# Sorted block attention and a PReLU FFN: unpadded q for batches 1 to 3, identity products up to the first FFN product, three banks for V of batch 0

## The chip, the cores and the metric

The kernel runs on one core of one Trainium2 chip. The metric is the device time of one launch in microseconds (us). TensorE is called PE, its weight loads PEld, VectorE DVE, ScalarE ACT, GpSimd POOL, and SyncE SP.

## The reference

There are 4 batches, 8 heads, 768 tokens and head size 64; tokens fall into 8 blocks of 96. A sorting matrix of 8 x 8 for each batch and head mixes the blocks of k and v; each block of q then attends to its own mixed block. The result, 3072 tokens of 512, goes through an FFN of width 2048.

```python
for _ in range(5):                       # P = sort_net, 8 x 8 per batch and head
    P = np.exp(P - np.max(P, axis=-1, keepdims=True))
    P = P / (np.sum(P, axis=-1, keepdims=True) + 1e-09)
    P = P / (np.sum(P, axis=-2, keepdims=True) + 1e-09)
k_sorted = np.einsum('bhij,bhjcd->bhicd', P, k_b)
v_sorted = np.einsum('bhij,bhjcd->bhicd', P, v_b)
scores = scale * np.matmul(q_b, k_sb.transpose(0, 1, 2, 4, 3))
attn = softmax(scores)
x = np.matmul(attn, v_sb)                # then to tokens x 512
h = x @ w_in                             # 3072 x 512 by 512 x 2048
g = np.maximum(h, 0.0) + alpha * np.minimum(h, 0.0)
return (g @ w_out).astype(np.float32)
```

## The kernel before

**Work in groups.** A group g is one block of one batch: g = 8 b + i, 32 groups in all, each with 8 heads. Batch 0 and the others ("far") go different ways. For each group `attention` issues: a score product of the 8 heads into the two psS banks (`s1`), a row maximum on DVE (into `nf` or `nm`), the exponential on ACT, an output product with V and a column of ones (`o`, into psO), a reciprocal and a multiplication on DVE (`xq`), and a turn of the result into `xT`. Group 1 uses psH and psYP in place of psS and psO. In batch 0 the scores are computed a second time with the operands exchanged, so that the exponential comes out turned already, and `xq` is turned on PE (`tr`). In the far batches the exponential `Esb` is turned into `ET` by a DMA transpose on SP's queue, and `xq` into `xT` by another.

**Operands.** `KT` holds the mixed k with 64 features of four heads in rows 0 to 63 and of the other four in rows 64 to 127. `prep_k` and `prep_v` mix k and v by products with the block matrix `BDK`, and copies on ACT or DVE empty the banks; `conv_v` first brings v into `VD`. q of batch 0 is brought into `QTz[0]` by `prep_q`. q of the far batches is loaded by eight POOL DMAs (`load_q`) into `QN`, in which each head has 128 columns, 64 with data and 64 of zeros, written once by eight POOL memsets; six DMA transposes (`turn_q`) of 128 x 1024 bring it into `QTz`, with 768 columns for each head. A far score product thus has 128 rows, of which 64 are zero, and 96 columns of weights; a score product of batch 0 has 64 rows and 128 columns of weights, of which the last 32 belong to the next block.

**FFN.** `ffn1` makes one of 16 parts of the hidden layer for up to four groups: four products into a psH bank, Relu on ACT, one DVE operation into `hT`. `ffn2` makes 128 tokens of output from `hT`, copies them to `outstg` and stores them from SP's queue. FFN work stands between the groups and fills PE.

**Order.** Nothing is ordered by hand. Every operation is entered with its engine, a planned duration, the keys that it reads and writes and a priority. `schedule` plays the operations through in planned time, `search` repeats this 1500 times with some priorities shifted at random and keeps the shortest plan, and `emit` writes each engine's instructions in that fixed order, with waits for what they need. A wait holds whatever stands behind it on the same engine.

**Filler.** After the plan is made, `fill` goes along PE's order and puts identity products into the gaps that the plan shows, 0.9 of each gap by the filler's unit (215 ns for a product of 512 columns). Their result in bank psY is not used. There are two stretches: from 5 us of planned time to the first V product that uses psY, and from the first FFN product to the first product of `ffn2`. A filler product waits for the identity matrix and stands in PE's order as any other.

```python
n = int((op.start - begin) * 0.9 / unit)
if op.start <= hi and n > 0:
    x = _Op("pe", lambda e, n=n: make(e, n), n * unit, 0.0, None, len(self.ops))
```

Of the lines that the profile names: L372 is any copy on ACT or DVE, L401 the loads of q, L409 its turns, L449 the memsets of `QN`, L515 the product that spreads the sorting matrices, L542 the products of q and k preparation, L565 the copy that pads `KT`, L585 those of V preparation, L622 the far scores, L625 the scores of batch 0 and L646 and L637 their second pass, L631 the row maximum, L658 the far exponential, L663 and L694 the DMA transposes to `ET` and `xT`, L669 the exponential of batch 0, L678 the output products, L686 `xq`, L701 its turn on PE, L723, L733 and L736 the first FFN layer on PE, ACT and DVE, L762 the second, L776 the stores, L877 the filler.

Of the kernel before, what the change touches and what calls it, by code (L numbers as in the profile page):

```python
# [24 lines left out]
BK0 = BLK + 16  # L25
NE = 3
# [34 lines left out]
class _Graph:  # L61
# [141 lines left out]
    def fill(self, make, unit, first, spans):  # L203

        out, last = [], self.ops[first].end + 300
        for op in self.order["pe"]:
            for lo, hi in spans:
                begin = max(last, lo)
                n = int((op.start - begin) * 0.9 / unit)
                if op.start <= hi and n > 0:  # L210
                    x = _Op("pe", lambda e, n=n: make(e, n), n * unit, 0.0, None, len(self.ops))
                    x.start, x.end = begin, begin + n * unit
                    x.deps.add(first)
# [76 lines left out]
def bass_sinkhorn_attn__then__act_prelu_kernel(  # L290
# [48 lines left out]
    QN = sb("QN", [128, 6, 8, 128], BF16)  # L339
# [3 lines left out]
    QTz = [sb("QTz%d" % n, [128, 2, 4, S], BF16) for n in range(2)]  # L343
# [51 lines left out]
    def load_q(b, prio):  # L395
        if b == 0:
            G.add(POOL, lambda e: e.dma_start(QS[0][:, :], AP(q.tensor, 0, [[3072, 128], [1, 3072]])),
                  load_us, w=[("QS", 0)], prio=prio, dma=(d_q[0], 0))
            return
        for h in range(H):  # L400
            G.add(POOL, lambda e, h=h: e.dma_start(  # L401
                AP(QN, h * 128 + (h // 4) * 64, [[6144, 128], [1024, 6], [1, 64]]),
                AP(q.tensor, b * HB + h * S * D, [[D, 128], [128 * D, 6], [1, D]])),
                660, r=[("QN0", h)] + paced(13, h // 2) * (b == 3), w=[("QN", h)], prio=prio,
                dma=(d_qn[h], 0))

    def turn_q(b, t, prio):
        n = b % 2
        G.add(SYNC, lambda e: e.dma_start_transpose(  # L409
            AP(QTz[n], t * 128, [[6144, 128], [768, 8], [1, 128]]),  # L410
            AP(QN, t * 1024, [[6144, 128], [1, 1024]])),
            4500, r=[("QN", h) for h in range(H)] + [("turned", 8 * b - 8 + t)] * (b > 1),
            w=[("QTzt", n, t)] + ([("Q0", u) for u in range(6)] + ["QTtail"] if n == 0 and t == 0 else []),
            prio=prio, dma=(d_qt[t], 0))
# [16 lines left out]
    def consts():  # L431
# [9 lines left out]
        G.add(DVE, lambda e: e.memset(AP(QTz[0], 3072, [[6144, 128], [1, 32]]), 0.0), 80, w=["QTtail"], prio=-60)  # L441
        G.add(DVE, lambda e: e.memset(AP(KT[0], 4 * NB * BK0, [[4 * NB * BK0 + 16, 128], [1, 16]]), 0.0), 80,
              w=["KTtail"], prio=-60)
        for n in range(2):
            G.add(DVE, lambda e, n=n: e.memset(AP(Es0[n], 768, [[800, 112], [1, 32]]), 0.0), 80, w=[("Etail", n)], prio=-60)
        for n in range(NE):
            G.add(DVE, lambda e, n=n: e.memset(AP(ET[n], 768, [[800, 128], [1, 32]]), 0.0), 80, w=[("ETtail", n)], prio=-21)
        for h in range(H):
            G.add(POOL, lambda e, h=h: e.memset(  # L449
                AP(QN, h * 128 + (1 - h // 4) * 64, [[6144, 128], [1024, 6], [1, 64]]), 0.0),  # L450
                400, w=[("QN0", h)], prio=-21)
# [96 lines left out]
    def prep_q(u, prio, bank):  # L548
        t, off, row, keys = bank
        G.add(PE, pairs(QS[0], 0, u, identb, 0, 128, bank), 372, r=[("QS", 0), "identb"], w=keys, prio=prio)  # L550
        o = AP(QTz[0], 8 * u, [[6144, 128], [96, 32], [48, 2], [1, 8]])
        i = AP(t, off, [[row, 128], [2, 32], [1, 2], [64, 8]])
        G.add(EITHER, lambda e: copy(e, o, i), t_either(512), r=keys, w=[("Q0", u)], prio=prio)
# [14 lines left out]

    first_y = []
# [7 lines left out]
    def prep_v(b, u, prio, bank=BANK_P):  # L577
        t, off, row, keys = bank
        n = b % 2

        def f(e):
            inst = None
            for dd in range(8):
                for th in range(2):
                    inst = e.matmul(AP(t, th * 64 * row + off + dd * 64, [[row, 64], [1, 64]]),  # L585
                                    AP(VD, (8 * u + dd) * 64, [[4096, 128], [1, 64]]),
                                    AP(BDK, b * 128 + th, [[512, 128], [2, 64]]))
            return inst
        op = G.add(PE, f, 374, r=[("VD", u), "VD0", ("BDK", b)], w=keys, prio=prio)
        if keys == ["psY"]:  # L590
            first_y.append(op)
        o = AP(VS[n], 8 * u, [[64 * 65, 112], [65, 64], [1, 8]])
        i = AP(t, off, [[row, 112], [1, 64], [64, 8]])
        G.add(EITHER, lambda e: copy(e, o, i), {"act": 685, "dve": 690}, r=keys + [("VS1", n)], w=[("VS", n, u)],
              prio=prio)

    d_e = [dma_sem("e%d" % n) for n in range(NE)]
    d_x = [dma_sem("x%d" % n) for n in range(NE)]

    def attention(g, prio):  # L600
# [14 lines left out]
        def s1(e):  # L615
            inst = None
            for h4 in range(4):
                for hp in range(2):
                    p = pos(h4, hp)
                    o = AP(psX, (p // 4) * 512 + (p % 4) * 96, [[1024, 96 if far else 128], [1, 96]])  # L620
                    if far:
                        inst = e.matmul(o, AP(QTz[n], hp * 3072 + h4 * 768 + i * 96, [[6144, 128], [1, 96]]),  # L622
                                        AP(KT[n], (h4 * 8 + i) * bk, [[ld, 128], [64, 2], [1, 48]]))
                    else:
                        inst = e.matmul(o, AP(QTz[n], hp * 64 * 6144 + h4 * 768 + i * 96, [[6144, 64], [1, 128]]),  # L625
                                        AP(KT[n], hp * 64 * ld + (h4 * 8 + i) * bk, [[ld, 64], [64, 2], [1, 48]]))
            return inst
        G.add(PE, s1, 395, r=kt_keys + qt_keys + [("xq", 1)] * (g == 2),
# [12 lines left out]
        def s2(e):  # L641
            inst = None
            for h4 in range(4):
                for hp in range(2):
# [3 lines left out]
                             AP(QTz[n], hp * 64 * 6144 + h4 * 768 + i * 96, [[6144, 64], [1, 96]]),  # L648
# [17 lines left out]
        else:  # L666
            G.add(PE, s2, 700, r=kt_keys + qt_keys + [("nm", m), "identb"],
                  w=banks_s, prio=ps_)
            G.add(ACT, lambda e: e.activation(  # L669
                AP(Es0[m], 0, [[800, nk], [384, 2], [1, 384]]),  # L670
                AP(psX, 0, [[1024, nk], [512, 2], [1, 384]]),
                ACTF.Exp), t_act(768), r=banks_s, w=[("Es0", m)], prio=ps_)

# [8 lines left out]
        G.add(PE, o, t_pe(*[(65, 65)] * 8), r=vs_keys + ([("ET", me), ("ETtail", me)] if far else [("Es0", m), ("Etail", m)]), w=banks_o, prio=prio)  # L682
# [111 lines left out]
    for u in range(8):  # L794
        prep_v(0, u, -45, (BANK_O + [BANK_P, BANK_Y])[u % 4])
# [78 lines left out]
    def warm(e, n):  # L874
        inst = None
        for _ in range(n):
            inst = e.matmul(psYP[:, 0, :], identb[:, :], AP(identb, 0, [[128, 128], [0, 4], [1, 128]]))  # L877
        return inst
    G.fill(warm, 215, ident_op, [(5000, first_y[0].start), (ffn_ops[0].start + 1, ffn_ops[1].start)])
# [40 lines left out]
```

## Time and profile before

| | |
|---|---|
| median of 3 runs | 254.17 us (253.9 to 256.3) |
| the profiled execution, its own time | 255.69 us |
| its span, first to last instruction | 254.0 us |
| PE busy | 235.3 us, 2679 products |
| DVE, ACT, POOL busy | 171.5, 160.5, 38.5 us |
| mean granted clock of PE | 0.987 |
| bytes moved | 32.17 MB |

The profile is of one execution; its span leaves out what lies before the first and after the last instruction. Busy time of PE counts overlapped products once each stretch, and products are pipelined, so the price of a group of products is read from its start to the start of the next. The granted clock is that of the throttle, 1.00 for full speed.

### The profile page before, as it was taken

How to read it: one execution, taken by the hardware profiler on the slowest of the kernel's cores; microseconds unless marked ns; L12 is line 12 of the kernel's file. 1: busy time of each engine (PE TensorE's matmuls, PEld its weight loads, DVE VectorE, ACT ScalarE, POOL GpSimd, SP SyncE). 2: the span in 40 equal slices, each digit the busy share in tenths (PEclk: the TensorE clock that was granted, in tenths of full speed). 3: DMA queues.
4: the chain of work that ended last, by engine and by line, in shares of the span. 5: the costliest groups of instructions: out<-in, count | busy, mean ns of one | idle time of the engine just before them, and what ended most of it. 6: DMA issues, size and time to landing. Idle time of an engine off the chain costs nothing.

```text
span 254.0 us, 6423 instructions
## 1 busy us (share of the span) xinstructions
PE 235.3 (93%) x2679; PEld 140.7 (55%) x2679; DVE 171.5 (68%) x347; ACT 160.5 (63%) x429; POOL 38.5 (15%) x63
## 2 busy tenths in 40 slices
PE   4796899989997978989899999999999999999995
PEld 1455678657654544556555555555555555555554
DVE  5887668796856775977885666656667765645530
ACT  4475446598866765878866485766677457534531
POOL 8995000000360011037000000000000000000000
PEclk9999589999999999999999999999999999999999
DMA  5999999999999999999979345233234433311103
GB/s 102 211 211 203 181 215 166 216 188 187 101 159 106 172 162 143 220 146 183 94 158 149 67 115 130 50 90 85 71 70 122 80 66 88 90 58 40 43 5 122
DMA packets 75534, 32.17 MB, mean 127 GB/s; under 512 B 67808, under 2 KB 71152, under 8 KB 75504
## 3 DMA queue, kind: packets, MB, share of 16 engines
q0 software_dynamic: 23632, 13.63, 41.1%
q1 hardware_dynamic: 51872, 18.11, 38.7%
q8 instruction: 21, 0.34, 0.6%
q14 instruction: 9, 0.07, 0.1%
HBM read 27.28 MB, written 6.29 MB: 132 GB/s over the span
## 4 chain that ended last, share of the span: by engine, by line
PE 75%; DVE 12%; DMA 9%; ACT 2%; issue 1%
PE psH L723 29%; PE psYP L762 26%; DMA ET<-Esb 8%; PE psS L762 3%; PE psO L678 3%; PE psS L622 3%; PE psYP L585 3%; PE psYP L542 2%; DVE hT L736 2%; DVE VD L372 2%; DVE VS L372 1%; PE psYP L877 1%; PE psS L637 1%; DVE KT L372 1%; ACT Esb L658 1%
## 5 line engine op out<-in xcount | busy, mean ns | idle before, releaser
L736 DVE SCALAR_TENSOR_TENSOR hT<-t,omaT,psH 128x384 bf16<-128x384 f32 (+1 forms) x139 | 77.5, 572 | 39.7 <-ACT t L733 38.1
L723 PE MATMUL psH<-xT,w_in_bf 128*128 128x384 bf16 (+1 forms) x556 | 98.5, 314 | 1.6 <-DVE hT L736 1.3
L733 ACT ACTIVATE t<-psH 128x384 f32<-128x384 f32 (+1 forms) x139 | 62.8, 466 | 44.5 <-PE psH L723 41.4
L762 PE MATMUL psYP<-w_out_bf,hT 128*128 128x512 bf16 x336 | 83.9, 379 | 1.0 <-DVE hT L736 0.6
L723 PEld LDWEIGHTS psH<-xT,w_in_bf 128*128 128x128 bf16 x556 | 50.8, 99 | 35.0 <-DVE hT L736 7.8
L658 ACT ACTIVATE Esb<-psS,nf 96x96 bf16<-96x96 f32 x192 | 46.3, 345 | 2.1 <-DVE nf L631 2.1
L762 PEld LDWEIGHTS psYP<-w_out_bf,hT 128*128 128x128 bf16 x336 | 30.7, 98 | 29.7 <-DVE hT L736 0.7
L401 POOL DMA_DIRECT2D QN<-in_q_dram x24 | 20.0, 857 | 45.2 <-DMA QTz<-QN 44.5
L631 DVE TENSOR_REDUCE nf<-psS 96x8 f32<-96x768 f32 x24 | 22.7, 948 | 3.9 <-PE psS L622 3.9
L686 DVE TENSOR_TENSOR xq<-psO,rec 96x512 bf16<-96x512 f32 x31 | 21.3, 686 | 1.0
L372 ACT ACTIVATE VS<-psYP 112x512 bf16<-112x512 f32 x17 | 11.7, 689 | 6.3 <-PE psYP L585 6.2
L372 ACT ACTIVATE outstg<-psYP 128x512 f32<-128x512 f32 x15 | 9.0, 597 | 9.9 <-PE psYP L762 9.8
L585 PE MATMUL psYP<-BDK,VD 128*64 128x64 bf16 x448 | 12.4, 198 | 1.9 <-DVE hT L736 1.0
L683 DVE RECIPROCAL rec<-psO 96x8 f32<-96x8 f32 x31 | 6.2, 201 | 11.7 <-PE psO L678 11.7
L877 PE MATMUL psYP<-identb 128*128 128x512 bf16 x34 | 10.6, 451 | 3.4 <-ACT identb L372 3.4
L585 PEld LDWEIGHTS psYP<-BDK,VD 128*64 128x64 bf16 x448 | 9.3, 111 | 6.9 <-issue 1.8
L622 PEld LDWEIGHTS psS<-KT,QTz 128*96 128x96 bf16 x192 | 11.7, 124 | 2.5
L678 PEld LDWEIGHTS psO<-VS,ET 112*128 112x128 bf16 x192 | 8.6, 98 | 7.6 <-DMA ET<-Esb 4.4
L622 PE MATMUL psS<-KT,QTz 128*96 128x96 bf16 x192 | 12.7, 209 | 0.0
L678 PE MATMUL psO<-VS,ET 112*128 112x65 bf16 x192 | 9.9, 194 | 2.8 <-DMA ET<-Esb 2.6
L372 DVE COPY VD<-VST 128x384 bf16<-128x384 bf16 x20 | 10.5, 565 | 1.4 <-DMA VST<-in_v_dram 1.4
L372 ACT ACTIVATE KT<-psYP 128x512 bf16<-128x512 f32 x11 | 6.6, 600 | 6.7 <-PE psYP L542 6.5
(115 smaller groups left out, 174.6 us busy)
## 6 DMA issues: line engine op xcount, KB each, us to landing
out_dram<-outstg SPq DMA_DIRECT2D x23, 256.0 KB, 2.2
KS<-in_k_dram POOLq DMA_DIRECT2D x3, 768.0 KB, 33.4
VST<-in_v_dram POOLq DMA_DIRECT2D x3, 768.0 KB, 29.1
QN<-in_q_dram POOLq DMA_DIRECT2D x24, 96.0 KB, 5.9
w_in_bf<-in_moe_w_in_dram POOLq DMA_DIRECT2D x4, 512.0 KB, 17.7
w_out_bf<-in_moe_w_out_dram POOLq DMA_DIRECT2D x2, 1024.0 KB, 28.4
QS<-in_q_dram POOLq DMA_DIRECT2D x1, 768.0 KB, 6.6
VST<-in_v_dram POOLq DMA_DIRECT2D x4, 192.0 KB, 4.6
```

The lines of the kernel that those rows point to most:

```text
L372: return e.activation(o, i, ACTF.Copy) if e is nc.scalar else e.tensor_copy(o, i)
L401: G.add(POOL, lambda e, h=h: e.dma_start(AP(QN, h * 128 + (h // 4) * 64, [[6144, 128], [1024, 6], [1, 64]]), AP(q.tensor, b * HB + h * S * ...
L585: inst = e.matmul(AP(t, th * 64 * row + off + dd * 64, [[row, 64], [1, 64]]), AP(VD, (8 * u + dd) * 64, [[4096, 128], [1, 64]]), AP(BDK, b ...
L622: inst = e.matmul(o, AP(QTz[n], hp * 3072 + h4 * 768 + i * 96, [[6144, 128], [1, 96]]), AP(KT[n], (h4 * 8 + i) * bk, [[ld, 128], [64, 2], ...
L631: G.add(DVE, lambda e: e.tensor_reduce(AP(nx, 0, [[8, 96], [4, 2], [1, 4]]), AP(psX, 0, [[1024, 96], [512, 2], [96, 4], [1, 96]]), AxisLis ...
L658: inst = e.activation(AP(Esb[me], p * 128, [[1024, 96], [64, 2], [1, 48]]), AP(psX, (p // 4) * 512 + (p % 4) * 96, [[1024, 96], [48, 2], [ ...
L678: inst = e.matmul(AP(psZ, hp * 512 + h4 * 68, [[1024, 128], [1, 65]]), AP(ET[me] if far else Es0[m], pos(h4, hp) * 96, [[800, nk], [1, 128]]),
L686: G.add(DVE, lambda e: e.tensor_tensor(out=AP(xq[me], 0, [[512, 96], [256, 2], [64, 4], [1, 64]]), in0=AP(psZ, 0, [[1024, 96], [512, 2], [ ...
L723: inst = e.matmul(AP(pt, poff, [[1024, 128], [1, n]]), AP(w_in_bf, kt * DFF + ft * 128, [[KT_TILES * DFF, 128], [1, 128]]), AP(xT, kt * XR ...
L733: G.add(ACT, lambda e: e.activation(AP(t1[tb], 0, [[384, 128], [1, n]]), AP(pt, poff, [[1024, 128], [1, n]]), ACTF.Relu, scale=-1.0), t_ac ...
L736: G.add(DVE, lambda e: e.scalar_tensor_tensor(out=AP(hT, ft * RING + tok % RING, [[FT_TILES * RING, 128], [1, n]]), in0=AP(t1[tb], 0, [[38 ...
L762: inst = e.matmul(AP(bank[0], bank[1], [[1024, 128], [1, n]]), AP(hT, ft * RING + tok % RING, [[FT_TILES * RING, 128], [1, 128]]), AP(w_ou ...
```

## The change

There are three parts. First, `QN` and `QTz` lose the zeros: in `QN` two heads share 128 columns, a turn moves 128 x 512 in place of 128 x 1024, and the far scores take the form that batch 0 has, with 64 rows and 128 columns of weights; two heads stand in the two halves of the rows and write to the two banks of psS. The eight POOL memsets go, each `QTz` gets a memset of 32 columns behind its end, and a far score product now also reads the 32 columns behind its block. The planned durations follow: 330 in place of 395 ns for a score product, 3000 in place of 4500 ns for a turn. Second, the filler's product has 256 columns (108 ns in the plan), and there are three stretches, each with what it waits for and its bank: to the output product of group 1 in psY, from there to the first FFN product in the first bank of psH (after the exponential of group 1, which reads psH), and from there to the first product of `ffn2` in psY. Third, since psY is now the filler's, `prep_v` of batch 0 goes round three banks in place of four. The search runs anew on the changed operations.

```diff
+QP = 4 * S + 32
...
-    def fill(self, make, unit, first, spans):
+    def fill(self, make, unit, spans):
-        out, last = [], self.ops[first].end + 300
+        out, last = [], 0.0
         for op in self.order["pe"]:
-            for lo, hi in spans:
-                begin = max(last, lo)
+            for lo, hi, deps, bank in spans:
+                begin = max([last, lo] + [self.ops[d].end + 300 for d in deps])
                 n = int((op.start - begin) * 0.9 / unit)
...
-    QN = sb("QN", [128, 6, 8, 128], BF16)
+    QN = sb("QN", [128, 6, 4, 128], BF16)
-    QTz = [sb("QTz%d" % n, [128, 2, 4, S], BF16) for n in range(2)]
+    QTz = [sb("QTz%d" % n, [128, QP], BF16) for n in range(2)]
...
-                AP(QN, h * 128 + (h // 4) * 64, [[6144, 128], [1024, 6], [1, 64]]),
+                AP(QN, h % 4 * 128 + (h // 4) * 64, [[3072, 128], [512, 6], [1, 64]]),
...
-            AP(QTz[n], t * 128, [[6144, 128], [768, 8], [1, 128]]),
-            AP(QN, t * 1024, [[6144, 128], [1, 1024]])),
-            4500, ...
+            AP(QTz[n], t * 128, [[QP, 128], [768, 4], [1, 128]]),
+            AP(QN, t * 512, [[3072, 128], [1, 512]])),
+            3000, ...
...
-        for h in range(H):
-            G.add(POOL, lambda e, h=h: e.memset(
-                AP(QN, h * 128 + (1 - h // 4) * 64, [[6144, 128], [1024, 6], [1, 64]]), 0.0),
-                400, w=[("QN0", h)], prio=-21)
...
-        pos = (lambda h4, hp: 2 * h4 + hp) if far else (lambda h4, hp: 4 * hp + h4)
+        pos = lambda h4, hp: 4 * hp + h4
...
-        qt_keys = [("QTzt", n, t) for t in range(i * 96 // 128, (i * 96 + 95) // 128 + 1)] if far else \
-            [("QTzt", n, t) for t in range(6)] + [("Q0", u) for u in range(6)] + ["QTtail"]
+        qt_keys = [("Qtail", n)] + ([("QTzt", n, t % 6) for t in range(i * 96 // 128, (i * 96 + 127) // 128 + 1)] if far else
+                                    [("QTzt", n, t) for t in range(6)] + [("Q0", u) for u in range(6)])
...
-                    o = AP(psX, (p // 4) * 512 + (p % 4) * 96, [[1024, 96 if far else 128], [1, 96]])
-                    if far:
-                        inst = e.matmul(o, AP(QTz[n], hp * 3072 + h4 * 768 + i * 96, [[6144, 128], [1, 96]]),
-                                        AP(KT[n], (h4 * 8 + i) * bk, [[ld, 128], [64, 2], [1, 48]]))
-                    else:
-                        inst = e.matmul(o, AP(QTz[n], hp * 64 * 6144 + h4 * 768 + i * 96, [[6144, 64], [1, 128]]),
-                                        AP(KT[n], hp * 64 * ld + (h4 * 8 + i) * bk, [[ld, 64], [64, 2], [1, 48]]))
+                    o = AP(psX, (p // 4) * 512 + (p % 4) * 96, [[1024, 128], [1, 96]])
+                    inst = e.matmul(o, AP(QTz[n], hp * 64 * QP + h4 * 768 + i * 96, [[QP, 64], [1, 128]]),
+                                    AP(KT[n], hp * 64 * ld + (h4 * 8 + i) * bk, [[ld, 64], [64, 2], [1, 48]]))
...
-        G.add(PE, s1, 395, ...
+        G.add(PE, s1, 330, ...
...
-        prep_v(0, u, -45, (BANK_O + [BANK_P, BANK_Y])[u % 4])
+        prep_v(0, u, -45, (BANK_O + [BANK_P])[u % 3])
...
-            inst = e.matmul(psYP[:, 0, :], identb[:, :], AP(identb, 0, [[128, 128], [0, 4], [1, 128]]))
+            inst = e.matmul(AP(t, off, [[row, 128], [1, 256]]), identb[:, :], AP(identb, 0, [[128, 128], [0, 2], [1, 128]]))
...
-    G.fill(warm, 215, ident_op, [(5000, first_y[0].start), (ffn_ops[0].start + 1, ffn_ops[1].start)])
+    out1, f1, f2 = warm_at["out"].start, ffn_ops[0].start, ffn_ops[1].start
+    G.fill(warm, 108, [(5000, out1, [ident_op], BANK_Y), (out1 + 1, f1, [warm_at["exp"].idx], BANK_H[0]),
+                       (f1 + 1, f2, [ident_op], BANK_Y)])
```

More of the change, by code (lines that the diff above doesn't have):

```diff
@@ L409, in turn_q @@
         G.add(SYNC, lambda e: e.dma_start_transpose(
[L410 to L413 removed]
+            AP(QTz[n], t * 128, [[QP, 128], [768, 4], [1, 128]]),
+            AP(QN, t * 512, [[3072, 128], [1, 512]])),
+            3000, r=[("QN", h) for h in range(H)] + [("turned", 8 * b - 8 + t)] * (b > 1),
+            w=[("QTzt", n, t)] + ([("Q0", u) for u in range(6)] if n == 0 and t == 0 else []),
             prio=prio, dma=(d_qt[t], 0))
@@ L588, in f @@
             return inst
-        op = G.add(PE, f, 374, r=[("VD", u), "VD0", ("BDK", b)], w=keys, prio=prio)
-        if keys == ["psY"]:
-            first_y.append(op)
+        G.add(PE, f, 374, r=[("VD", u), "VD0", ("BDK", b)], w=keys, prio=prio)
         o = AP(VS[n], 8 * u, [[64 * 65, 112], [65, 64], [1, 8]])
@@ L668, in attention @@
                   w=banks_s, prio=ps_)
-            G.add(ACT, lambda e: e.activation(
+            op = G.add(ACT, lambda e: e.activation(
                 AP(Es0[m], 0, [[800, nk], [384, 2], [1, 384]]),
@@ L681, in o @@
             return inst
-        G.add(PE, o, t_pe(*[(65, 65)] * 8), r=vs_keys + ([("ET", me), ("ETtail", me)] if far else [("Es0", m), ("Etail", m)]), w=banks_o, prio=prio)
+        op = G.add(PE, o, t_pe(*[(65, 65)] * 8), r=vs_keys + ([("ET", me), ("ETtail", me)] if far else [("Es0", m), ("Etail", m)]), w=banks_o, prio=prio)
+        if g == 1:
+            warm_at["out"] = op
         G.add(DVE, lambda e: e.reciprocal(AP(rec[m], 0, [[8, 96], [4, 2], [1, 4]]),
```

25 lines of the change are left out of this document (14 added, 11 removed).

## The prediction

> **What bounds the kernel now.** I read the page's busy shares and its row of granted clock first, then a table of stretches, because a share of the whole span mixes stages that wait for different things.
>
> ```profile
> PE 235.3 (93%) x2679; PEld 140.7 (55%) x2679; DVE 171.5 (68%) x347; ACT 160.5 (63%) x429; POOL 38.5 (15%) x63
> PEclk9999589999999999999999999999999999999999
> 8.00:13.00 5.00, 3.50 (x105) 2.33 (x106) 4.02 (x16) 2.90 (x7) 4.48 (x12) 1.00 1.04 214
> 13.00:18.00 5.00, 4.97 (x142) 3.02 (x143) 4.08 (x9) 3.60 (x7) 4.93 (x8) 1.00 1.06 215
> 18.00:22.30 4.30, 2.89 (x96) 2.31 (x96) 4.30 (x7) 3.53 (x6) 4.30 (x7) 1.00 1.07 214
> 22.30:27.60 5.30, 3.21 (x84) 2.40 (x84) 2.90 (x8) 2.22 (x4) 0.52 (x1) 0.91 1.07 175
> 27.60:37.00 9.40, 9.38 (x97) 6.99 (x96) 5.81 (x16) 4.16 (x11) 0.00 (x0) 0.69 1.22 207
> 37.00:62.00 25.00, 23.27 (x427) 16.62 (x426) 20.62 (x47) 18.32 (x40) 0.00 (x0) 1.00 1.39 187
> 62.00:130.00 68.00, 62.42 (x771) 37.26 (x768) 50.57 (x91) 51.07 (x149) 17.44 (x24) 1.00 1.29 150
> 130.00:250.00 120.00, 119.98 (x953) 67.36 (x951) 73.97 (x126) 71.07 (x201) 0.00 (x0) 1.00 0.36 82
> ```
>
> The columns of the stretches are: stretch, its length, busy microseconds (and instructions) of PE, PEld, DVE, ACT and POOL, granted clock, DMA share, GB/s. Four things are to be seen. From 130 us on PE has no idle time at all (119.98 of 120), so there each microsecond of products saved is a microsecond of the kernel. From 37 to 130 us PE idles 1.7 + 5.6 = 7.3 us; there work saved on PE counts only as far as those waits do not grow. From 27.6 to 37 us PE is full, but at a clock of 0.69: work at a slow clock, not waiting. Before that PE waits for DVE and ACT (18 to 22.3 us: DVE busy 4.30 of 4.30).
>
> **Scores of batches 1 to 3 (the largest term).** Batch 0 already multiplies in the 64-row form, so the trace holds both prices. First come the weight loads and products of the padded form and of the 64-row form, then each form with the product that follows it, from the timeline of PE (start, length, instruction).
>
> ```profile
> L622 PEld LDWEIGHTS psS<-KT,QTz 128*96 128x96 bf16 x192 | 11.7, 124 | 2.5
> L625 PEld LDWEIGHTS psS<-KT,QTz 64*128 64x128 bf16 x56 | 1.5, 98 | 0.5 <-issue 0.3
> 62.00:130.00 68.00, 6.36 (x96) 5.80 (x96) 1.00 1.29 150
> 130.00:220.00 90.00, 6.37 (x96) 5.85 (x96) 1.00 0.43 94
> ...
> 148.44 0.56 PE L622 MATMUL psS<-KT,QTz 128*96 128x96 bf16 x8
> 148.83 1.46 PE L723 MATMUL psH<-xT,w_in_bf 128*128 128x384 bf16 x8
> ...
> 53.67 0.34 PE L625 MATMUL psS<-KT,QTz 64*128 64x96 bf16 x8
> 53.95 0.44 PE L585 MATMUL psYP<-BDK,VD 128*64 128x64 bf16 x16
> ...
> 17.39 0.34 PE L625 MATMUL psH<-KT,QTz 64*128 64x96 bf16 x8
> 17.57 0.33 PE L625 MATMUL psS<-KT,QTz 64*128 64x96 bf16 x8
> ```
>
> The lengths overlap with what follows, so a group's price is the distance to the next start: 148.83 - 148.44 = 0.39 us padded, 53.95 - 53.67 = 0.28 us in the 64-row form when a 128-row product follows, and 17.57 - 17.39 = 0.18 us when another 64-row group follows. In the new kernel mostly 128-row products follow, so I take 0.28: 0.11 us saved per group. There are 24 groups (192 products of eight), 12 of them up to 130 us and 12 behind: 12 x 0.11 = 1.3 us in the full stretch, which must show, and 1.3 us before it. Term: **-2.6 us**. Bounds: 1.3 (only the full stretch counts) and 24 x (0.39 - 0.18) = 5.0.
>
> The Trainium skill, "TensorE: Matmul & The Clock Gate", section "Part 3: Packing small matmuls — row/col tiling", says that products in different row groups run concurrently, about 4 ns apart in start. The 17.39 row fits it better than the 53.67 row; by it the group is four pairs of 40 ns, an estimate of 0.16 us, and the kernel would come to an estimated 246.5 us.
>
> **The first FFN products (second term).** The next rows are the slow stretch in the chain that ended last (start, length, what), and two windows of PE alone (length, PE busy, clock, DMA share, GB/s).
>
> ```profile
> 26.80 0.50 ACT xT L372
> 27.68 1.39 PE psH L723 x8
> ...
> 30.90 1.28 PE psYP L877 x3
> 32.62 1.14 PE psH L723 x8
> ...
> 38.31 0.66 PE psH L723 x8
> 25.40:26.40 1.00, 0.34 (x4) 1.00 1.01 103
> 27.60:33.00 5.40, 5.40 (x45) 0.50 1.22 199
> ```
>
> PE is busy 0.34 of the microsecond ahead of 26.4 us, then the clock is granted at half and stays there until about 33 us: eight products of L723 take 1.39 and 1.14 us there and 0.66 us later. The old filler stops at the first V product that uses psY; the new one goes on to the first FFN product, partly in the bank psH, so the clock should not fall. Of the 5.40 us at clock 0.50, three identity products (L877) make 1.28; the remaining 4.1 us would take half: **-2.0 us**. Upper bound, by the clock of the two stretches of the table: 5.30 x 0.09 + 9.40 x 0.31 = 3.4. Lower bound 0: DVE and ACT (the xT copy that ends at 27.30, then the Relu and the hT operation behind each product) may take over as what ends last.
>
> **What the filler and three banks cost.** Identity products stand in order on PE; a product of scores, output or V that becomes ready early waits behind them, and DVE and ACT wait for it. The planner fills 0.9 of each gap that it computes. The trace has three gaps before such products in this stretch, and the copies that empty the V banks:
>
> ```profile
> 20.50 1.27 DVE L372 CAST VS<-psYP 112x512 bf16<-112x512 f32 x2
> 22.32 0.45 PE L585 MATMUL psYP<-BDK,VD 128*64 128x64 bf16 x16 [0.82 <-DVE VS L372]
> 22.81 0.69 ACT L372 ACTIVATE VS<-psYP 112x512 bf16<-112x512 f32 x1 [0.83 <-PE psYP L585]
> 25.58 0.34 PE L701 MATMUL psO<-identb,xq 96*128 96x96 bf16 x4 [0.77 <-DVE xq L686]
> 26.42 0.34 PE L701 MATMUL psYP<-identb,xq 96*128 96x96 bf16 x4 [0.49 <-DVE xq L686]
> ```
>
> A V product waits for a copy even with four banks (0.82 at 22.32), and a copy takes 1.27 / 2 = 0.64 to 0.69 on either engine; with three banks the eighth product waits at most for one more copy, 0.69. An overrun of the filler costs at most the tenth left plus one unit in each gap. From that I take **+0.3 us** for both, between 0 and 2.0 (one copy, and a whole gap of 0.77 plus 0.49).
>
> **Loads and turns of q.** Eight POOL memsets go. They took this long; what stood behind them on POOL was the issue of the q loads and the copy that pads KT:
>
> ```profile
> 8.71 3.83 POOL L449 MEMSET QN<- 128x384 bf16 x8
> 16.07 0.83 POOL L565 COPY KT<-KT 128x512 bf16<-128x512 bf16 x1
> 46.63 16.95 SPq L409 DMA_TRANSPOSE QTz<-QN  x6
> ```
>
> The pad copy ended at 16.90 and the first scores began at 17.39: 0.49 us of cover, so nothing; without it an earlier copy would be a gain. The q data come behind other loads (175 to 215 GB/s in the table) and reached the SP queue at 46.63; an earlier issue does not bring them earlier: nothing, and nothing lost, since the queue's order stays. The turns move half the columns. The nearest rows are the landing times:
>
> ```profile
> ET<-Esb SPq DMA_TRANSPOSE x24, 3.0
> xT<-xq SPq DMA_TRANSPOSE x24, 2.4
> QTz<-QN SPq DMA_TRANSPOSE x18, 4.6
> PE psO L678 <- DMA ET<-Esb: 2.6, 3, 1.3
> ```
>
> ET and xT differ by half the columns as the two turns will, and by 0.6 us of landing. Who gains is the ET transposes that share SP and the DMA engines with the turns: PE waited 2.6 us for them, three times. I take **-0.5 us**, between 0 and -2.6. The extra reads (block 3 of a batch now also reads turned tile 3, block 7 tile 0 again, and the tail memsets) wait for nothing: the six turns of batch 1 are issued by 63.6 us, those of batches 2 and 3 a batch ahead.
>
> **Sum.** -2.6 - 2.0 - 0.5 + 0.3 = -4.8 us. The profiled execution took 255.69 us (span 254.0 and 1.7 around it): 250.9 by its own time. It lies 1.5 above the median of the runs, 254.17, from which the same sum gives **249.4 us**.
>
> **Rivals.**
>
> *The early gain is swallowed.* PE gets ahead between 27 and 130 us and waits longer for copies and DMA (DMA share above 1 up to 130 us in the table). Only the 12 late groups count: 254.2 - 1.3 = 252.9. For it: 7.3 us of idle PE in that stretch. Against it: DVE is busy 50.57 and ACT 51.07 of 68, so neither is the bound.
>
> *The change does not hold the clock.* The filler works from planned gaps; if the real ones fall after its products, PE idles and the clock drops as before: 254.2 - 2.6 - 0.5 + 0.3 = 251.4. Against it: before 22 us a sparser filler held 1.00.
>
> *Wider weights cost more.* The scores load 128 columns in place of 96. If a load goes by columns, the group takes 0.39 x 128/96 = 0.52 us, 24 x 0.13 = 3.1 us more in place of 2.6 less: 249.4 + 5.7 = 255.1. Against it: 98 ns for the 128-column load and 124 for the 96-column one, above. This is the rule of the Trainium skill, "TensorE: Matmul & The Clock Gate", section "LDWEIGHTS (loading the stationary operand)", a time proportional to columns; the trace disagrees here, and the same page's section on weight-path modes says that a full 128-column load is faster.
>
> *Slower: PE starves in the middle.* All costs and keys differ, so the planner's search settles on another order. If in that order the ET transposes and copies of batches 1 and 2 end later against the products that stand in PE's order, the idle time of 37 to 130 us grows. Should it double, +7.3 - 4.8 = +2.5: 256.7. It decides from 4.8 us of added idle PE. For it, from the chain that ended last:
>
> ```profile
> 72.87 7.11 DMA ET<-Esb
> ```
>
> So an ET transpose can take 7.11 us beside a median of 3.0. Against it: the turns that share its queue shrink.
>
> *Cold filler.* If the clock falls while the filler runs, each unit takes twice its planned time. From 8 to 27.6 us PE was idle 5.0 us, which 0.9 of the filler at double time would overrun by 0.8 x 5.0 = 4.0; with the clock's gain gone too, 249.4 + 2.0 + 4.0 = 255.4. Against it: clock 1.00 up to 22.3 us.
>
> **How the numbers follow.** Forecast 0.66, swallowed 0.10, clock not held 0.07, wider weights 0.02, starving 0.12, cold filler 0.03. About 1% (2.5 us) is what a measurement of this kernel can tell from no change. Of the forecast 0.61 lies below 251.6 and 0.05 within 1%; of the clock case 0.05 and 0.02; swallowed, wider weights and cold filler are within; starving is slower. Together faster 0.66, same 0.22, slower 0.12. The range goes from 245.8 to 255.2. Below, the scores' upper bound takes 2.4 more off the forecast, and of what the clock and the ET waits can still give (1.4 + 2.1) I add a third, 1.2. Above, it takes in swallowed, clock and wider weights and leaves out starving and the cold filler. The forecast's own range is 246.5 to 251.6.
>
> **What would show it.** Right: PEclk without the 5 and the 8; the first L723 groups of eight at 0.66 us; score groups of 64 rows, 0.28 us to the next start; QTz landing near 4 us or less; PE full from 130 us on, and ending earlier. Wrong: more idle PE between 37 and 130 us than 7.3, or a first FFN product later than 27.6 us.

## The result and the profile after

The changed kernel takes 251.13 us in the median of 4 runs (249.56 to 251.74) beside 255.24 for the kernel before. The ratio is 0.9856, 95% interval 0.9809 to 0.9903. A second measurement of the same kernel gave 251.33 us and 0.9899 (0.9853 to 0.9945). Both intervals leave out 1: it is faster, by 1.0 to 1.4%, where 1.9% was forecast. The profiled execution took 251.64 us (span 249.9), 4.05 us less than the one before. Ratios and intervals leave out runs more than 1.5% above the fastest of their kernel, among them the profiled executions of the padded kernel and of the changed kernel with seed 8; where a median and a ratio differ below, that is why.

The first view of the page, the row of granted clock, and the same stretches as before (length, busy time and instructions of PE, PEld, DVE, ACT, POOL, clock, DMA share, GB/s). Line numbers differ from kernel to kernel; the tile names tell which operation a row is.

```profile
PE 235.9 (94%) x2743; PEld 139.8 (56%) x2743; DVE 173.1 (69%) x350; ACT 159.5 (64%) x427; POOL 35.8 (14%) x55
PEclk9999999799999999999999999999999999999999
18.00:22.30 4.30, 4.09 (x115) 2.93 (x107) 3.55 (x7) 3.94 (x6) 1.21 (x3) 1.00 1.06 213
22.30:27.60 5.30, 5.01 (x89) 3.52 (x83) 3.39 (x8) 1.99 (x4) 0.00 (x0) 1.00 1.03 169
27.60:37.00 9.40, 9.40 (x141) 7.26 (x138) 7.16 (x19) 5.44 (x14) 0.00 (x0) 1.00 1.24 209
37.00:62.00 25.00, 21.64 (x375) 15.32 (x372) 18.23 (x41) 16.08 (x34) 0.00 (x0) 0.93 1.42 186
62.00:130.00 68.00, 65.71 (x816) 37.18 (x811) 54.02 (x99) 53.07 (x156) 18.39 (x24) 1.00 1.18 133
130.00:250.00 120.00, 117.23 (x948) 63.56 (x945) 73.76 (x126) 69.25 (x196) 0.00 (x0) 1.00 0.31 77
```

The clock holds at 1.00 from 22 to 37 us: the filler does what it should. But between 37 and 62 us PE now idles 3.36 us (1.7 before) and the clock falls there instead (0.93). Between 62 and 130 us PE idles 2.3 us where it was 5.6. So the time came from the stretch behind 62 us. The waits of PE and two rows of its timeline name both:

```profile
PE psYP L539 <- DMA KS<-in_k_dram: 2.5, 1, 2.5
PE psO L670 <- DMA ET<-Esb: 0.2, 1, 0.2
...
28.54 0.83 PE L717 MATMUL psH<-xT,w_in_bf 128*128 128x192 bf16 x8
...
41.69 0.44 PE L539 MATMUL psYP<-BDK,KS 64*64 64x64 bf16 x16 [2.50 <-DMA KS<-in_k_dram]
```

The load of k of batch 1, issued at 8.17 us, lands at 41.6 us, and the order has its first product where PE arrives at 39.2. The first FFN product comes at 28.54 us, where it was 27.61. How far the FFN had come: by 41.5 us 48 products of the first layer and 8 of the second (before: 60 and 8); by 62 us 108 and 24 (before: 112 and 24); by 130 us 284 and 122 (before: 271 and 112). All of the lead is made between 62 and 130 us. Of ET the 2.6 us of waiting are down to 0.2.

The far scores now take the form of batch 0, at the distance to the next start that the prediction read there. The timeline of PE, a group and what follows it:

```profile
148.82 0.34 PE L615 MATMUL psS<-KT,QTz 64*128 64x96 bf16 x8
149.09 0.44 PE L580 MATMUL psYP<-BDK,VD 128*64 128x64 bf16 x16
```

That is 0.27 us to the next start, against 0.39. It is not yet what a group costs, because the products ahead of it change too; the kernels with wide turns below show that.

### The profile page after: what moved, and what is told of

Its sections match the earlier page's. It is cut to its first block, busy times and chain, and to the rows that moved or that the text cites. A ratio compares the mean times of both kernels' runs of the same rounds, so it can differ in the third digit from the quotient of the medians.

```text
span 249.9 us, 6561 instructions
## 1 busy us (share of the span) xinstructions
PE 235.9 (94%) x2743; PEld 139.8 (56%) x2743; DVE 173.1 (69%) x350; ACT 159.5 (64%) x427; POOL 35.8 (14%) x55
## 3 DMA queue, kind: packets, MB, share of 16 engines
q1 hardware_dynamic: 42656, 15.76, 31.6%
## 4 chain that ended last, share of the span: by engine, by line
PE 73%; DMA 15%; DVE 5%; POOL 3%; ACT 2%; issue 1%; POOLq 0%
PE psH L717 30%; PE psYP L756 28%; DMA KS<-in_k_dram 13%; PE psS L756 3%; PE psS L615 3%; PE psO L670 3%; PE psYP L539 2%; DMA ET<-Esb 2%; PE psYP L580 2%; DVE hT L730 2%; DVE xq L680 1%; ACT t L727 1%; POOL w_in_bf L791 1%; ACT Esb L648 1%; PE psO L756 1%; DVE nf L621 1%
## 5 line engine op out<-in xcount | busy, mean ns | idle before, releaser
L756 PE MATMUL psYP<-w_out_bf,hT 128*128 128x512 bf16 x336 | 85.3, 380 | 0.0
L717 PEld LDWEIGHTS psH<-xT,w_in_bf 128*128 128x128 bf16 x556 | 49.7, 98 | 32.9 <-DVE hT L730 5.2
L402 POOL DMA_DIRECT2D QN<-in_q_dram x24 | 20.5, 887 | 45.8 <-DMA QTz<-QN 40.6
L872 PE MATMUL psYP<-identb 128*128 128x256 bf16 x83 | 12.8, 297 | 3.4 <-ACT identb L373 3.4
L580 PE MATMUL psYP<-BDK,VD 128*64 128x64 bf16 x416 | 11.5, 198 | 0.8 <-ACT VS L373 0.8
L580 PEld LDWEIGHTS psYP<-BDK,VD 128*64 128x64 bf16 x416 | 8.6, 111 | 5.5 <-issue 1.9
L539 PE MATMUL psYP<-BDK,KS 64*64 64x64 bf16 x304 | 8.5, 197 | 3.2 <-DMA KS<-in_k_dram 2.5
L373 ACT ACTIVATE outstg<-psYP 128x512 f32<-128x512 f32 x13 | 7.8, 600 | 5.0 <-PE psYP L756 4.8
L872 PEld LDWEIGHTS psYP<-identb 128*128 128x128 bf16 x83 | 8.0, 106 | 5.1 <-ACT identb L373 3.4
L615 PE MATMUL psS<-KT,QTz 64*128 64x96 bf16 x248 | 10.8, 207 | 0.0
L539 PEld LDWEIGHTS psYP<-BDK,KS 64*64 64x64 bf16 x304 | 6.4, 111 | 7.6 <-issue 4.7
## 6 DMA issues: line engine op xcount, KB each, us to landing
KS<-in_k_dram POOLq DMA_DIRECT2D x3, 768.0 KB, 33.4
```

The costliest lines, as they stand in the source:

```text
L373: return e.activation(o, i, ACTF.Copy) if e is nc.scalar else e.tensor_copy(o, i)
L402: G.add(POOL, lambda e, h=h: e.dma_start(AP(QN, h % 4 * 128 + (h // 4) * 64, [[3072, 128], [512, 6], [1, 64]]), AP(q.tensor, b * HB + h * ...
L539: inst = e.matmul(AP(t, hp * 64 * row + off + c * 64, [[row, 64], [1, 64]]), AP(src, hp * 64 * 3072 + cc * 64, [[3072, 64], [1, 64]]), AP( ...
L717: inst = e.matmul(AP(pt, poff, [[1024, 128], [1, n]]), AP(w_in_bf, kt * DFF + ft * 128, [[KT_TILES * DFF, 128], [1, 128]]), AP(xT, kt * XR ...
L756: inst = e.matmul(AP(bank[0], bank[1], [[1024, 128], [1, n]]), AP(hT, ft * RING + tok % RING, [[FT_TILES * RING, 128], [1, 128]]), AP(w_ou ...
L872: inst = e.matmul(AP(t, off, [[row, 128], [1, 256]]), identb[:, :], AP(identb, 0, [[128, 128], [0, 2], [1, 128]]))
```

## Experiments

**Theories.** 1: the scores and the shorter turns make the gain; the filler gains nothing, since the k load holds PE back at 41.6 us. 2: the filler makes it. 3: the order that the search drew makes it. Where a kernel has "its own order" of the changed kernel, the list of operations and planned durations is left alone, so that the search draws the same order, and only what an operation emits is changed.

| kernel | median us (runs) | ratio to before | interval | idle PE 37 to 62 us | 62 to 130 us |
|---|---|---|---|---|---|
| before | 254.2 (31) | 1 | | 1.7 | 5.6 |
| changed | 251.13 (4), 251.33 (6) | 0.9856, 0.9899 | 0.9809–0.9903, 0.9853–0.9945 | 3.4, 2.9 | 2.3, 2.5 |
| q alone | 254.01 (10) | 0.9975 | 0.9931–1.0018 | 1.8 | 5.0 |
| filler and banks alone | 256.15 (10) | 1.0077 | 1.0034–1.0121 | 2.6 | 5.3 |
| changed order, old filler | 250.04 (4) | 0.9837 | 0.9745–0.993 | 1.1 | 3.3 |
| changed order, padded q | 255.71 (10) | 0.999 | 0.9941–1.0039 | 2.4 | 6.1 |
| changed order, wide turns | 256.31 (10) | 1.0072 | 1.0031–1.0113 | 2.7 | 7.5 |
| changed order, k first | 249.66 (4), 251.01 (6) | 0.9821, 0.9877 | 0.9744–0.9898, 0.9825–0.9929 | 1.1, 3.1 | 3.4, 2.2 |
| the same, old filler | 250.79 (6) | 0.9873 | 0.983–0.9917 | 0.9 | 3.1 |
| changed, seed 8 | 254.03 (10) | 0.9985 | 0.9946–1.0024 | 3.6 | 3.9 |
| before, seed 8 | 253.86 (10) | 0.9969 | 0.9934–1.0004 | 2.2 | 4.1 |
| changed, seed 9 | 252.02 (12) | 0.9926 | 0.9892–0.996 | 3.6 | 2.1 |

Each ratio is to the runs of the kernel before on the same chip; its own median there was 254.2 to 255.2 us. The padded kernel, the one with wide turns and the two of seed 8 ran on another chip than the rest. The idle times are from one profiled execution of each, by the same stretches as above.

**Each part alone.** The first kernel has only the edits of q, the second only those of the filler and the banks; each is planned anew.

```diff
 # q alone: the kernel before with QN, QTz, load_q, turn_q, s1 and their durations as changed
 # filler and banks alone: the kernel before with fill, warm and prep_v(0, ...) as changed
```

> Only the first part of the change (q unpadded, scores of 64 rows, narrow turns) on the kernel before; the filler and the four banks stay. The planner searches anew. Theory 1 (the gain is that of the scores and of the shorter turns, behind 62 us): the ratio to the kernel before is 0.985 to 0.99, as large as that of the whole change, and the clock still falls to half between 26 and 33 us. Theory 2 (the gain is that of the filler): within 0.3% of before. Theory 3 (the order that the search drew makes the gain): any ratio between 0.98 and 1.02.

> Only the second and third part of the change (filler of 256 columns up to the first FFN product, three banks for V of batch 0) on the kernel before; q stays padded. The planner searches anew. Theory 1: within 0.5% of before, since the data of the second k load (landed at 41.6 us in the changed kernel) hold back what follows, so that what the filler gains is waited off there. Theory 2: 2 to 4 us faster. Theory 3: any ratio between 0.98 and 1.02.

Neither part carries the gain alone: q alone 0.9975, filler alone 1.0077, slower. Theory 2 falls. Theory 1 in its plain form falls as well, since q alone was to give the whole (0.985 to 0.99) and the filler alone was to stay within 0.5% of before. Both kernels drew orders of their own, in which PE idles 5.0 and 5.3 us behind 62 us, as in the kernel before; so the next kernels hold the order still.

**The old filler in the changed order.**

```diff
-    G.fill(warm, 108, [(5000, out1, ...), (out1 + 1, f1, ...), (f1 + 1, f2, ...)])
+    G.fill(warm, 215, [(5000, v_ops[3].start, [ident_op], BANK_Y), (f1 + 1, f2, [ident_op], BANK_Y)])
```

> The changed kernel with its own order on every engine, but with the filler of the kernel before: units of 512 columns, which end at the fourth V product, and then from the first FFN product to the first of the second layer. Three banks stay. Theory 1: at 41.6 us PE waits for k of batch 1 as in the changed kernel, the clock falls to half between about 26 and 33 us as in the kernel before, and the time is within 1 us of the changed kernel. Theory 2: 2 to 3 us slower than the changed kernel.

Stretches of PE alone (length, busy, clock, DMA share, GB/s):

```profile
22.30:27.60 5.30, 3.31 (x77) 0.71 1.06 167
27.60:37.00 9.40, 9.20 (x88) 0.62 1.24 211
37.00:62.00 25.00, 23.88 (x440) 1.00 1.40 182
62.00:130.00 68.00, 64.68 (x791) 1.00 1.11 136
```

The clock falls as before (0.62 from 27.6 to 37 us), and the kernel is as fast as the changed one: 0.9837 against 0.9856 and 0.9899. What the slow clock takes, idle time gives back: 1.1 us of it from 37 to 62 in place of 3.4, and by 62 us it has done 116 products of the first FFN layer where the two profiled executions of the changed kernel have done 108 and 116. The eleventh `hT` operation on DVE starts at 40.6 us here and at 38.0 and 38.3 in the changed kernel, the sixteenth at 48.0 against 49.4 and 47.7: what the new filler wins is gone by then. The wait for k of batch 1, which Theory 1 expected here too, is not in this trace.

**Padded q, and wide turns, in the changed order.** Both write the zeros in the operation that clears part of VD, ahead of the weight loads. In the second the scores stay in 64 rows, and a turn moves 512 more columns that nothing reads as data.

```diff
 # padded q: as the kernel before
+            AP(QTz[n], t * 128, [[QP, 128], [768, 8], [1, 128]]), AP(QN, t * 1024, [[6144, 128], [1, 1024]])
+            inst = e.matmul(o, AP(QTz[n], hp * 3072 + h4 * 768 + i * 96, [[QP, 128], [1, 96]]), ...)
 # wide turns: the turn of the kernel before, the scores of the changed one
+            AP(QTz[n], t * 128, [[QP, 128], [768, 8], [1, 128]]), AP(QN, t * 1024, [[6144, 128], [1, 1024]])
```

> The changed kernel with its own order on every engine and its filler, but with q padded as in the kernel before: wide turns, score products of 128 rows and 96 columns of weights, and the zeros of q written by POOL ahead of the weight loads. Theory 1 (scores and turns make the gain): 3 to 4 us slower than the changed kernel, that is back at the kernel before, with each score group 0.11 us longer. Theory 3 (the order that the search drew makes most of the gain): 1 to 2.6 us slower than the changed kernel, the price of the score groups alone (24 x 0.11 us), and still faster than the kernel before.

> The changed kernel with its own order and its score products of 64 rows, but each turn of q moves 128 x 1024 as before, half of it zeros that nothing reads. If the shorter turns are worth something of themselves: ET transposes land later and the idle time of PE between 62 and 130 us goes from 2.3 back towards 5.6 us, 1 to 3 us slower than the changed kernel. If not: within 0.7 us of it. Theory 3 expects the latter.

With the turns wide again the whole gain is gone, with either form of scores; Theory 3, which expected little of the turns, falls in this order. Here is the place in the kernel with wide turns: stretches (columns as in the first table), the chain that ended last, and PE's row:

```profile
80.00:89.40 9.40, 8.16 (x117) 4.48 (x112) 8.11 (x14) 7.71 (x24) 1.08 (x2) 1.00 0.88 130
89.40:100.00 10.60, 5.36 (x45) 2.48 (x44) 3.06 (x7) 2.11 (x7) 1.06 (x2) 0.68 1.11 161
...
86.16 8.10 DMA ET<-Esb
94.30 0.62 PE L672 MATMUL psO<-VS,ET 112*128 112x65 bf16 x8 [4.88 <-DMA ET<-Esb]
```

and the same place in the changed kernel:

```profile
80.00:89.40 9.40, 8.17 (x134) 4.83 (x135) 8.18 (x15) 7.69 (x22) 1.08 (x2) 1.00 0.83 114
89.40:100.00 10.60, 9.63 (x132) 5.04 (x129) 7.70 (x14) 7.81 (x28) 2.12 (x4) 1.00 0.82 124
...
84.73 5.34 DMA ET<-Esb
90.12 0.42 PE L670 MATMUL psO<-VS,ET 112*128 112x65 bf16 x8 [0.20 <-DMA ET<-Esb]
```

PE reaches this output product at 89.4 us in the one and 89.9 in the other. With narrow turns the transpose that it needs has been issued at 84.73 and takes 5.34 us; with wide ones it is issued at 86.16 and takes 8.10. PE then waits 4.88 us in place of 0.20, and over the stretch from 89.4 to 100 us the granted clock is 0.68. The wide kernel takes longer even where the clock holds: its one run at a mean clock of 1.00 took 255.25 us, where the changed kernel's four at 1.00 took 249.56 to 250.62.

The delay begins earlier, in a buffer that is used again. Six turns of batch 1, the loads of q of batch 2 into the same `QN`, and the first turn of batch 2, with wide turns and then in the changed kernel:

```profile
46.81 16.52 SPq L410 DMA_TRANSPOSE QTz<-QN  x6
65.54 7.16 POOL L402 DMA_DIRECT2D QN<-in_q_dram  x8 [42.28 <-DMA QTz<-QN]
78.50 1.23 SPq L410 DMA_TRANSPOSE QTz<-QN  x1
...
46.64 13.86 SPq L410 DMA_TRANSPOSE QTz<-QN  x6
62.61 7.30 POOL L402 DMA_DIRECT2D QN<-in_q_dram  x8 [40.55 <-DMA QTz<-QN]
75.45 1.19 SPq L410 DMA_TRANSPOSE QTz<-QN  x1
```

The loads wait for the last turn of batch 1 to land, so longer turns put them off by 2.93 us and the next batch's first turn by 3.05, and the transposes to `xT` and `ET` stand behind that turn on SP's queue. All of the loss lies in this part: from the 41st to the 61st `hT` operation the wide kernel takes 41.7 us and the changed one 35.0 and 35.1 in its two profiles. From there to the end they take the same, 131.9 us against 132.0 and 131.9. SP's queue (q1) moved 18.11 MB in 51872 packets with wide turns and 15.76 MB in 42656 with narrow ones:

```profile
q1 hardware_dynamic: 51872, 18.11, 36.0%
```

```profile
q1 hardware_dynamic: 42656, 15.76, 31.6%
```

(The first row is of wide turns, the second of the changed kernel: packets, MB, share of 16 engines.) The order of both wide kernels was drawn for short turns. So the 4.4 us are what long turns cost in this order; short turns in the order of the kernel before were not run.

Between the two wide kernels the 64-row form shows no gain: 0.999 padded, 1.0072 in 64 rows, with intervals that just overlap. The traces say why. Behind 123 us (124 in 64 rows) both run the same groups of products in the same order, and PE is busy all the time. From one product of the first layer to the last group of the second, padded first (columns as in the first table):

```profile
123.00:242.66 119.66, 119.66 (x1006) 68.34 (x1002) 82.37 (x140) 76.30 (x219) 1.65 (x2) 1.00 0.41 89
124.02:243.58 119.56, 119.56 (x1007) 64.55 (x1002) 82.34 (x140) 76.40 (x219) 1.04 (x2) 1.00 0.40 86
```

Fourteen score groups in 64 rows save 0.10 us together. The start of a group and of its neighbours shows where the rest goes, in the kernel before and in the changed one:

```profile
181.94 1.03 PE L762 MATMUL psYP<-w_out_bf,hT 128*128 128x512 bf16 x4
182.81 0.52 PE L622 MATMUL psS<-KT,QTz 128*96 128x96 bf16 x8
183.17 1.03 PE L762 MATMUL psYP<-w_out_bf,hT 128*128 128x512 bf16 x4
184.03 0.81 PE L723 MATMUL psH<-xT,w_in_bf 128*128 128x384 bf16 x4
...
169.94 1.03 PE L756 MATMUL psYP<-w_out_bf,hT 128*128 128x512 bf16 x4
170.90 0.34 PE L615 MATMUL psS<-KT,QTz 64*128 64x96 bf16 x8
171.18 1.04 PE L756 MATMUL psYP<-w_out_bf,hT 128*128 128x512 bf16 x4
172.06 0.81 PE L717 MATMUL psH<-xT,w_in_bf 128*128 128x384 bf16 x4
```

The score group shrinks from 0.36 to 0.28 us, but the four products ahead of it take 0.96 in place of 0.87 and those behind it 0.88 in place of 0.86: 2.12 us for the three in place of 2.09. Over the fourteen groups of the two wide kernels the groups themselves are 1.54 us shorter, the products ahead of them 1.34 us longer and those behind 0.11 longer. A group gains, 0.08 to 0.10 us, only in the four places where products of 64 columns follow it.

Both wide kernels also delay the copy that pads KT: PE waits 1.4 and 1.5 us for it at 18 us. By 62 us they have done 115 products of the first layer, where the changed kernel has done 108 and 116, so the delay is gone by then.

**k of batch 1 first.** The two POOL loads change places in the finished plan.

```diff
+    po[x], po[y] = po[y], po[x]      # second half of w_out, k of batch 1
```

> The changed kernel with its own order on every engine, except that POOL issues the load of k of batch 1 ahead of the second half of w_out instead of behind it. Theory 1 (the wait of 2.5 us for this load at 41.6 us takes back what the filler gains): the load lands by about 37 us, the wait of PE goes, the clock holds at 1.00 from 37 to 62 us in every run, and the kernel takes 2 to 4 us less than the changed kernel. Rival (later waits, for copies and transposes, set the end of that stretch anyway): the wait goes and reappears between 45 and 130 us, and the time is within 1 us of the changed kernel.

> The changed kernel with its own order and the load of k of batch 1 ahead of the second half of w_out, unedited since its first run, with more runs. Theory 1: 1 to 2.5 us faster than the changed kernel beside it, about 249.7 us, with most runs at clock 1.00. Rival (later waits take it back): within 0.7 us of the changed kernel.

> The changed kernel once more, unedited, with more runs beside the next three on one chip. Theory 1 and its rivals: ratio to the kernel before of 0.98 to 0.99, and runs in steps of about 1.7 us by how many stretches of 3.4 us the clock spends at half.

The wait for k goes in both profiles. The clock does not hold in every run, though: four of the ten have a mean of 0.986 or 0.993. In the first measurement the kernel took 249.66 us, in the second 251.01 beside 251.33 for the changed kernel; the intervals overlap widely, so no gain is shown. Theory 1's 2 to 4 us were not there. The rival saw it right. In the second profile another wait stands in its place,

```profile
52.26 1.04 PE L756 MATMUL psYP<-w_out_bf,hT 128*128 128x512 bf16 x4 [1.83 <-DVE hT L730]
```

1.83 us for the hidden layer from DVE, and by 62 us 111 products of the first layer are done.

**k first with the old filler.**

```diff
+    po[x], po[y] = po[y], po[x]
+    G.fill(warm, 215, [(5000, v_ops[3].start, [ident_op], BANK_Y), (f1 + 1, f2, [ident_op], BANK_Y)])
```

> The changed kernel with its own order, with the load of k of batch 1 ahead of the second half of w_out, and with the filler of the kernel before. Theory 1 (the new filler is worth its 2 us only where the k load does not hold PE back): 1.5 to 3 us slower than the same kernel with the new filler, that is 251 to 253 us. Rival (the filler is worth nothing here even then, since the first FFN product comes later with it): within 0.7 us of the kernel with the new filler.

250.79 us against 251.01: the filler gains nothing even without the wait for k. The stretches of PE, old filler first, then new:

```profile
27.60:37.00 9.40, 9.21 (x93) 0.65 1.15 207
37.00:62.00 25.00, 24.13 (x450) 1.00 1.41 185
```

```profile
27.60:37.00 9.40, 9.12 (x136) 1.00 1.15 206
37.00:62.00 25.00, 21.86 (x403) 1.00 1.44 181
```

With the clock lost PE idles 0.9 us between 37 and 62; with the clock held it idles 3.1. So in these two profiles what the faster clock saves between 37 and 62 us comes back as waiting.

**Other seeds.** The only edit is the seed of the search.

```diff
-        rng = random.Random(7)
+        rng = random.Random(8)      # and 9
```

> The changed kernel with another seed for the planner's search (8 in place of 7), nothing else. Theory 1: within 1 us of the changed kernel. Theory 3: 1 to 4 us away from it, to either side, with other idle time of PE between 37 and 130 us.

> The kernel before with the same other seed. Theory 1: within 1 us of the kernel before, and 3 to 4 us behind the changed kernel with that seed. Theory 3: 1 to 4 us away from the kernel before, and the distance to the changed kernel of that seed is not the 3.6 us of the first seed.

> The changed kernel with a third seed (9) for the planner's search. Theory 3 (the drawn order is worth as much as the change): 250 to 256 us, at least 1.5 us away from the changed kernel or from its seed 8. Theory 1: within 1 us of the changed kernel.

With seed 8 the changed kernel takes 254.03 us and the kernel before 253.86 (0.9985 and 0.9969): no gain at all. With seed 9 the changed kernel takes 252.02 (0.9926). Three draws of the changed kernel spread over 2.9 us, nearly the size of the change, and not by the clock alone: the runs at a mean clock of 1.000 took 249.56 to 250.62 us with seed 7, 251.01 to 252.92 with seed 9 and 252.44 to 253.53 with seed 8. So Theory 3 holds in this form: the draw counts for about as much as the change. Its other guess, that the kernel before would move by 1 to 4 us with the seed, missed: it moved by 0.3, as Theory 1 had it, which in turn missed the distance of 3 to 4 us between the two kernels of seed 8. Seed 9 fits both, within 1 us of the changed kernel and 2.0 from its seed 8. What in a draw does it is not shown; the profiled executions idle 2.3, 3.9 and 2.1 us behind 62 us (seeds 7, 8, 9), which is not the order of their times. And the draw is not all, for in the one order that was held still the narrow turns make the difference.

## Why the prediction was right, step by step

The forecast of 249.4 us lies 1.7 us under the first measured median, inside the range, with the sign right. That the number came out near is in good part luck. The two largest terms, -2.6 for the scores and -2.0 for the first FFN products, gave nothing that the runs show. The gain came with the turns, at which only -0.5 was put, and in an order that the search happened to draw: with seed 8 the same change gains nothing. One of the two things that were to show the prediction wrong did happen, a first FFN product later than 27.6 us (28.54); the other did not, as PE idles 5.7 us between 37 and 130 us and not more than 7.3.

- **Scores, -2.6 us.** This step failed, though the distance was read right: 0.27 to 0.28 us to the next start in place of 0.36 to 0.39. That distance is not the price, because the products ahead of a 64-row group take 0.10 us longer. The 1.3 us of the last stretch, which "must show", were 0.10 us for fourteen groups in one order. The row of batch 0 had it already: the output products ahead of the score group at 53.67 us took 0.34 us from 53.33 on, where those of another group took 0.24 from 24.16 on. The Trainium skill, "TensorE: Matmul & The Clock Gate", section "Part 3: Packing small matmuls — row/col tiling", with its 4 ns between concurrent products, had led to an estimate of 0.16 us; the trace has 0.27, and the measurement decides.
- **First FFN products, -2.0 us.** This step failed. The clock did hold (1.00 from 22 to 37 us); the gain did not come. The lower bound of 0 and the rival "the early gain is swallowed" describe it: PE waited 2.5 us at 41.6 for a k load whose landing I had not looked up (the page's list of DMA issues gave 33.4 us from issue to landing for such a load), and with that load moved up it waited elsewhere in the same stretch.
- **Filler and three banks, +0.3 us.** Too small. The first FFN product came 0.93 us later. The last V product and the last copy of V, in the timeline of the changed kernel, show most of it:

```profile
23.60 0.44 PE L580 MATMUL psO<-BDK,VD 128*64 128x64 bf16 x16
24.08 0.69 ACT L373 ACTIVATE VS<-psO 112x512 bf16<-112x512 f32 x1 [0.90 <-PE psO L580]
```

  ACT waits 0.90 us for the last V product, and the last copy starts at 24.08 where the kernel before began its last at 23.37. That is 0.7 us, the "one more copy" (0.69) that I had set as the bound and then weighed down. With the old filler in the same order the first FFN product came at 28.5 as well, so it is not the filler's. Whether it is the banks or the order was not separated. By 62 us it no longer counted.
- **Turns, -0.5 us (0 to -2.6).** The direction was right, the size and the path were not. Narrow against wide turns in one order is 1.7% of the kernel (0.9899 against 1.0072), 4.4 us, on two chips and each against the kernel before: one wait of 4.88 us in place of 0.20, and the clock that falls behind it. I had looked at the q loads of batch 1 alone and found "nothing, and nothing lost"; the loads of batch 2 wait for the turns of batch 1, since both use `QN`. And I had taken the landing times of the old order (2.6 us of waits in three places) for the bound; in another order one transpose had more to lose.
- **The draw.** I had it only as the slower rival ("PE starves in the middle"). Its size, some 3 us from draw to draw of the changed kernel, is as large as the change.

## What to carry to other kernels

Where a planner draws the order anew, compare an edit in the order held still and over several seeds; here the draws lay 2.9 us apart, and the change was worth 2.6 to 3.7 us in one draw and nothing in another. Price a short group of products together with the products ahead of it and behind it, not by the distance to the next start alone. A saving on a busy engine counts only up to the next fixed arrival, so look for the loads and transposes that land next before booking it. Where a transfer empties a buffer that is loaded again, its length sets when those loads start, and with them everything that stands behind them on a queue.

## What the runs showed of the hardware

Products of 64 rows between products of 128 rows make those ahead of them longer: four products of 512 columns take 0.96 us to the next start ahead of a 64-row group and 0.86 to 0.87 ahead of a padded one, in every such place of the changed kernel and of the kernel before behind 125 us. What in PE takes these 0.10 us the profile does not show.

Idle time of PE can cost twice, by the wait and by the clock behind it. The ten runs of the changed kernel fall by their mean granted clock: 249.56, 249.94, 250.43 and 250.62 us at 1.00; 251.26 to 251.78 us (five) at 0.993; 252.10 at 0.986. A mean of 0.993 over 250 us is 0.007 x 250 / 0.5 = 3.5 us at half clock, in which about 1.7 us of products are lost; the means of the first two groups are 1.4 us apart. The profiles have the stretches at half clock themselves: 3.41 us in the changed kernel (43.75 to 47.16 us), 6.83 in the kernel before, 10.24 with q alone, one, two and three times the first. A wait of one length is followed by such a stretch in one execution and not in another. The changed kernel's first profile has it behind a wait of 2.50 us for k, and its second, with the same wait 1.97 us long, has a clock of 1.00 throughout; 1.83 us of idle PE have it behind them with the filler alone (at 82.5 us) and not with k first (at 50.4 us). The Trainium skill, "TensorE: Matmul & The Clock Gate", section "Part 1: The HAM clock gate (the "warmup" mystery)", says that the clock is decided over free-running windows of 3.4 us; the stretches of 3.41 us and its multiples agree with it.

In several kernels PE stood still in the first 30 us for reasons that the profile does not show. The longest, in the kernel with q alone:

```profile
23.68 0.22 PE L583 MATMUL psYP<-BDK,VD 128*64 128x64 bf16 x2 [2.48 <-issue]
```

This pause of 2.48 us was not traced to a cause; in the two profiles of the changed kernel such pauses before 30 us are 0.4 and 0.9 us together.
